# Six of sixteen weight parts converted behind the transform, three load buffers for the first tile, stage one of a batch spread over a batch, low parts subtracted in halves

## The chip, the cores and the metric

The kernel runs on one core of one Trainium2 chip. The metric is device microseconds of one execution; lower is better. A core has TensorE (PE: matmuls, and PEld: loading of their weights), VectorE (DVE), ScalarE (ACT) and GpSimd (POOL). All DMAs of this kernel are issued by SyncE (SP) or by GpSimd. Each engine works through its own list of instructions in order.

## The reference

The input x has 8 batches of 3008 tokens with 256 numbers each. Per batch there is a Fourier transform over the tokens, a complex linear layer with soft thresholding on the spectrum, and an inverse transform. Then all 24064 tokens go through a network with squared ReLU:

```
X = rfft(x, axis=1)
Yr = Xr @ w_r - Xi @ w_i + b_r
Yi = Xr @ w_i + Xi @ w_r + b_i
Yr, Yi = sign(Y) * max(abs(Y) - 0.01, 0)
y = irfft(Yr + 1j * Yi, n=3008, axis=1)
g = max(y @ w_in, 0) ** 2        # w_in: 256 x 2048
out = g @ w_out                  # w_out: 2048 x 256
```

w_in and w_out arrive as 64-bit numbers, and the kernel makes its own 32-bit pairs of them: a high part that TensorE's fast 32-bit format holds, and a low part that is the rest. A product is then three matmuls: high x high, low x high, high x low.

## The kernel before, in words

**The transform** splits 3008 into 64 x 47. Stage one (`Fwd`, `Fwd32`) folds the two halves of the input (one sum, one difference), multiplies both by the constant matrix `am32` and stores the result through the buffer `xe` to s1 in memory. Stage two works on frequency groups: it loads `ka` from s1, multiplies by `bm` (`psf<-kbb,ka` or `psf<-kb,ka`), mixes with w_r and w_i, shrinks (three VectorE operations: add the bias, clamp, subtract), transforms back and stores the high and low parts `kuh` and `kul` to s3. Stage three (`Back`) loads `du` from s3 in three DMAs (L419 to L424), multiplies by `dx_sb` (L432, L435, L436) and adds the results into `yr`, the tokens of one tile.

**The front.** Batch 0 is done ahead of everything else and in full 32-bit matmuls: seven blocks of stage one (`ring`, L596), then 24 units (`units`, class `Unit32`, L355), one per group. Meanwhile the weights are made. They come in 16 parts of 512 KB (`parts`, L598): eight of w_in, eight of w_out, ordered as they are needed. A part (`Double`, L125) is loaded into `dst`, and then one ScalarE and six VectorE operations of 512 columns turn the 64-bit numbers into `dw` (`bits`, `join`). A part of w_out is then split into its halves (`split`, one ScalarE copy, one VectorE subtraction); for two parts of w_in `win_sums` adds four sums and splits seven blocks. The loop at L619 lays out units and parts together: part n is loaded at unit n * 13 // 10 - 1 and converted at n * 13 // 10 + 3 (L611), all 16 within the 24 units.

**The main part.** The tokens make 48 tiles of 504 or 500 tokens (`HALF` holds half a tile), six per batch. A tile's `Tokens` make four sums and differences (`ms`) of the tokens and split seven blocks into `yt0` and `yt1`, on ScalarE (high) and GpSimd (low). Then eight `Step`s per tile: `first` and `second` do seven products with `win` instead of eight (a Strassen-Winograd scheme; 21 matmuls into `psh`), VectorE combines them to `mc`, ScalarE does ReLU, square and the high part `mg0`, GpSimd subtracts the low part `mg1` (L532, one operation of 1008 or 1000 columns per step). `out` (L534) multiplies by `wout` and adds into two banks `pso0` and `pso1`, one for each half of the 256 output columns: six matmuls per call, d outside, the three terms inside. At the last step each bank is copied to `mo` (one buffer) and stored.

**Order.** The steps' own instructions are chained per engine by `then` (L453). The loop at L648 counts slots m, two per step, 96 per batch. Everything else is laid out as jobs with dates in slots: the pairs of groups of the next batch (`pair_tasks`), stage one of the batch after that (`fwd_tasks`, L568: load at -2.5, fold at -0.8, matmul and store at +0.3 from its date) and stage three and the tokens of the next tile (`back_tasks`, L575). For batch b + 2, stage one stands at slots 75 to 92, one unit every 1.4 slots (L659). A scheduler then orders the instructions of each engine by a simulation; instructions traced earlier have precedence when several could start. `issue_after` puts an instruction behind another one on its engine. All DMAs made by `load_next` on SP are one chain. The stretch between the front and the first step is the hand-over: `back_tasks(0, 0)` loads three `du` with one buffer (`MAIN`, L39) and makes the first tile. The front's memory pool is closed at L636 and the main part's opened in the same memory.

The banks of TensorE's results: while the steps run, `psh` has four, `pso` two, and `psf` two, which stage one, the pairs and stage three share.

Of the kernel before, what the change touches and what calls it, by code (L numbers as in the profile page):

```python
# [31 lines left out]
NF = FF // 128  # L32
LAM = 0.01
NP1 = N1 + 1
FRONT = {
    "a32": 1, "b32": 1, "w320": 1, "w321": 1, "big": 5, "small": 6, "ds": 1, "dw": 4, "ka": 5, "xe": 4,
    "kv": 3, "psf": 6,
}
MAIN = {  # L39
# [17 lines left out]
def fnet_moe(ctx: ExitStack, tc, x, w_r, w_i, b_r, b_i, w_in, w_out, bm, cm, dx, a32, c32, out):  # L57
# [14 lines left out]
    wout = [const.tile([128, NF, D], F32R, name=f"wout{j}") for j in range(2)]  # L72


    front = ExitStack()
    phase = {"pool": front.enter_context(tc.tile_pool(name="front", bufs=2)), "bufs": FRONT}
    phase["psum"] = front.enter_context(tc.tile_pool(name="front_ps", bufs=2, space=PSUM))

    def T(name, shape, dt, tag=None):
        tag = tag or name  # L80
        return phase["pool"].tile(shape, dt, name=name, tag=tag, bufs=phase["bufs"].get(tag, 2))
# [43 lines left out]
    class Double:  # L125
# [7 lines left out]
        def bits(self, after):  # L133
# [5 lines left out]
            with tc.issue_after(after.done.ins):  # L139
                act.activation(a, top.bitcast(F32), AF.Abs, scale=2.0 ** -112)  # L140
            with tc.issue_after(after.cut.ins):
# [18 lines left out]
    def halves(hi, lo, v, eng):  # L160
        copy(act, hi, v)
        sub(eng, lo, v, hi)
# [247 lines left out]
    class Back:  # L410
# [45 lines left out]

    class Tokens:
        def __init__(self, t):
            self.t, self.h = t, tiles[t][2]

        def sums(self, k):
            y, h = raw[self.t], self.h
            b11, b21 = y[:, 0, :h], y[:, 1, :h]
            if k == 0:
                self.s = T("ms", [128, 4 * HM], F32)[:, :4 * h].rearrange("p (j h) -> p j h", j=4)
            t1, t3, t2, t4 = (self.s[:, j] for j in range(4))
            if k == 0:
                sub(pool, t1, y[:, 0, h:2 * h], b11)
                sub(pool, t3, y[:, 1, h:2 * h], y[:, 0, h:2 * h])
            else:  # L470
                pool.tensor_add(out=t2, in0=b11, in1=t3)
                sub(pool, t4, b21, t2)

        def split(self, k):
            y, h = raw[self.t], self.h
            if k == 0:
                yts[self.t] = [
                    T(f"yt{j}", [128, 7 * HM], F32R)[:, :7 * h].rearrange("p (j h) -> p j h", j=7) for j in range(2)
                ]
            yh, yl = yts[self.t]  # L480
            if k == 0:
                halves(yh[:, B11], yl[:, B11], y[:, 0, :h], pool)
            elif k == 1:
                two = y[:, 1, :2 * h].rearrange("p (j h) -> p j h", j=2)
                halves(yh[:, B21:B22 + 1], yl[:, B21:B22 + 1], two, pool)
            else:
                j = 2 * (k - 2)
                halves(yh[:, T1 + j:T1 + j + 2], yl[:, T1 + j:T1 + j + 2], self.s[:, j:j + 2], pool)


    acc = {}
# [1 line left out]
    class Step:  # L493
# [24 lines left out]
        def second(self):  # L518
            h, c = self.h, self.c
            pc, pd = self.ps[2:]  # L520
            self.product(pc[:, 0], S4, B22)
            self.product(pc[:, 1], A22, T4)
            self.product(pd[:, 0], A12, B21)
            then(dve, dve.tensor_add, out=c[:, 1:3], in0=pc, in1=self.v)
            then(dve, dve.tensor_add, out=c[:, 0], in0=pd[:, 0], in1=self.p1)
            self.g = g = [
                T(f"mg{j}", [128, 4 * HM], F32R)[:, :4 * h].rearrange("p (j h) -> p j h", j=4) for j in range(2)
            ]
            then(act, act.activation, c, c, AF.Relu)
            then(act, act.activation, c, c, AF.Square)  # L530
            then(act, copy, act, g[0], c)
            then(pool, sub, pool, g[1], c, g[0])  # L532

        def out(self, j):  # L534
            t, h, f = self.t, self.h, 2 * self.n + j
            if f == 0:
                acc[t] = [bank([128, 512], f"pso{d}") for d in range(2)]
            for d in range(2):
                dsl = slice(d * 128, d * 128 + 128)
                for k, (w, g) in enumerate(((0, 0), (1, 0), (0, 1))):  # L540
                    then(
                        pe, pe.matmul, acc[t][d][:, :2 * h], wout[w][:, f, dsl],
                        self.g[g][:, 2 * j:2 * j + 2].rearrange("p j h -> p (j h)"),
                        start=f == 0 and k == 0, stop=f == NF - 1 and k == 2,
                    )
            if f == NF - 1:
                b, c0, _ = tiles[t]
                for d in range(2):
                    o = T("mo", [128, 2 * HM], F32)[:, :2 * h]
                    then(act, copy, act, o, acc[t][d][:, :2 * h])  # L550
                    nc.sync.dma_start(out[b, :, d, c0:c0 + 2 * h], o)
                del acc[t]
# [22 lines left out]
    def back_tasks(t, start):  # L575
        b, c0, h = tiles[t]
        new = range(-(-c0 // W2), -(-(c0 + 2 * h) // W2))
        jobs = []
        for j, q in enumerate(new):
            k, at = Back(b, q), start + 2.6 * j  # L580
            jobs += [(at, k.load), (at + 1.6, k.mm)]
            if len(k.spans) > 1:
                jobs += [(start + 15.6, k.put)]
        k = Tokens(t)
        for j in range(2):
            jobs += [(start + 8.1 + j, lambda j=j: k.sums(j))]
        for j in range(4):
            jobs += [(start + 10.1 + 1.2 * j, lambda j=j: k.split(j))]
        return jobs

    def at(items, n, *names):
# [14 lines left out]
        at(ring, r - 1, "put")  # L606
    with tc.issue_after(ring[2].last.ins):
        load_mix_weights()
    extra = []
    for n, p in enumerate(parts):  # L610
        k = n * 13 // 10  # L611
        extra += [(k - 1, p.load), (k + 3, lambda p=p, u=units[k]: p.bits(u)), (k + 3, p.join)]
# [4 lines left out]
    extra.sort(key=lambda j: j[0])  # L617
    last = units[2]
    for r in range(-5, len(units) + 3):  # L619
        at(units, r + 5, "load")  # L620
        at(units, r + 1, "fwd", "bins")
        at(units, r - 1, "shrink")
        at(units, r - 2, "back", "store")
        at(units, r, "mix")
        while extra and extra[0][0] <= r:
            job = extra.pop(0)[1]
            if job.__name__ == "load":
                with tc.issue_after(last.get.ins):
                    job()
                last = job.__self__  # L630
            else:
                job()
# [3 lines left out]
    front.close()  # L636
    phase.update(
        pool=ctx.enter_context(tc.tile_pool(name="main", bufs=2)), bufs={**MAIN, "psf": 2},
        psum=ctx.enter_context(tc.tile_pool(name="main_ps", bufs=1, space=PSUM)),
    )  # L640

    pairs = [[Pair(b, j) for j in range(G // 2)] for b in range(B)]
    steps = [Step(t, n) for t in range(len(tiles)) for n in range(NF // 2)]
    slots = len(HALF) * NF
    for _, job in sorted(back_tasks(0, 0), key=lambda j: j[0]):
        job()
# [113 lines left out]
```

## Time and profile before

| | |
|---|---|
| median of 3 runs | 2750.51 us (2748.16 to 2753.14) |
| the profiled execution | 2752.96 us |
| its span, first to last instruction | 2751.2 us |
| granted TensorE clock, mean | 0.978 |
| busy PE / PEld | 2614.5 / 2362.4 us |
| busy DVE / ACT / POOL | 1748.7 / 1663.6 / 1635.3 us |
| first block of stage two on PE | 38.03 us |
| last store of batch 0 issued | 141.77 us |
| first long row of step matmuls | 166.99 us |

Times in the profile are microseconds from the first instruction. A row of the timeline has the start, the time that the row covers, engine, line, operation, out<-in and the count; in brackets stands how long the engine was idle before it and what released it. "SPq" rows are DMA issues. A row of the groups has the count, the busy time in us and the mean ns of one, and behind the second bar the idle time before. A row of the windows has the busy time of each engine in a stretch. A row of the waits has who waited for whom, the total us, how often, and the longest.

### The profile page before, as it was taken

What the parts mean: (1) busy time and instruction counts of PE and PEld (TensorE: products, weight loads), DVE (VectorE), ACT (ScalarE), POOL (GpSimd) and SP (SyncE); (2) the same over time, 40 slices, a digit from 0 to 9 for tenths busy, and PEclk for the clock granted to TensorE, in tenths of its full rate; (3) what the DMA queues carried; (4) which work ended last, traced back from release to release, by engine and by line L of the source; (5) the groups of instructions that cost most, each with busy time, mean ns of one, the idle gap of its engine ahead of it and who ended that gap; (6) DMA issues with size and microseconds to landing.
All of it is one profiled execution on the core that took longest, in us unless ns stands there. A gap on an engine that the chain in (4) does not pass through costs nothing.

```text
span 2751.2 us, 47098 instructions
## 1 busy us (share of the span) xinstructions
PE 2614.5 (95%) x16856; PEld 2362.4 (86%) x16856; DVE 1748.7 (64%) x3787; ACT 1663.6 (60%) x2434; POOL 1635.3 (59%) x1282
## 2 busy tenths in 40 slices
PE   5779999899999999999999999999999999999998
PEld 3669889789988898889988899889998889988987
DVE  5935666477755777567764677547775577665554
ACT  3446656566666666656665666656766666665665
POOL 3456556556566656655666565665656566665553
PEclk8979999999999999999999999999999999999999
DMA  8432333323332232323333332332333233221000
GB/s 249 160 111 79 95 93 108 108 82 91 95 109 87 85 96 82 108 87 95 87 89 98 96 88 85 105 94 86 90 92 109 80 94 92 72 62 45 26 16 16
DMA packets 191260, 250.48 MB, mean 91 GB/s; under 512 B 21755, under 2 KB 135667, under 8 KB 191027
## 3 DMA queue, kind: packets, MB, share of 16 engines
q1 hardware_dynamic: 178627, 224.85, 26.7%
q0 software_dynamic: 12400, 22.61, 3.8%
q8 instruction: 135, 2.21, 0.3%
q14 instruction: 98, 0.80, 0.1%
HBM read 146.85 MB, written 100.53 MB: 90 GB/s over the span
## 4 chain that ended last, share of the span: by engine, by line
PE 75%; POOL 6%; DVE 5%; ACT 4%; issue 3%; DMA 2%; POOLq 0%; SPq 0%; DVEq 0%; ACTq 0%
PE pso L455 33%; PE psh L455 27%; PE psf L293 6%; POOL mg L92 2%; PE psf L228 2%; PE psf L325 2%; PE psf L272 2%; ACT mc L455 2%; DVE kv L314 1%; DVE mc L455 1%; DMA du<-s 1%; POOL xs L207 1%; POOL yt L92 1%; PE psf L436 1%; PE psf L435 1%
## 5 line engine op out<-in xcount | busy, mean ns | idle before, releaser
L92 POOL TENSOR_TENSOR mg<-mc,mg 128x1000 fp32r<-128x1000 f32 (+1 forms) x384 | 912.5, 2376 | 620.7 <-ACT mg L88 619.6
L455 PE MATMUL pso<-mg,wout 128*128 128x500 f32 (+1 forms) x4608 | 1167.3, 395 | 20.1 <-POOL mg L92 13.8
L455 PE MATMUL psh<-yt,win 128*128 128x250 f32 (+1 forms) x8064 | 1102.5, 283 | 14.3 <-ACT yt L88 12.5
L455 PEld LDWEIGHTS psh<-yt,win 128*128 128x128 f32 x8064 | 1035.0, 190 | 55.3 <-ACT yt L88 15.7
L455 ACT ACTIVATE mc<-mc 128x1000 f32<-128x1000 f32 (+1 forms) x768 | 802.6, 1045 | 374.9 <-DVE mc L455 365.5
L455 PEld LDWEIGHTS pso<-mg,wout 128*128 128x128 f32 x4608 | 832.0, 190 | 170.2 <-POOL mg L92 21.7
L455 DVE TENSOR_TENSOR mc<-psh,mv 128x500 f32<-128x500 f32 (+3 forms) x768 | 419.4, 548 | 573.3 <-PE psh L455 538.7
L88 ACT CAST mg<-mc 128x1000 fp32r<-128x1000 f32 (+1 forms) x384 | 396.8, 1033 | 17.4
L455 DVE TENSOR_TENSOR mv<-psh,mu 128x500 f32<-128x500 f32 (+1 forms) x384 | 260.6, 679 | 37.5 <-PE psh L455 5.7
L89 DVE COPY mp<-psh 128x250 f32<-128x250 f32 (+1 forms) x384 | 159.7, 416 | 88.4 <-PE psh L455 72.1
L293 PE MATMUL psf<-wx,kxh 128*128 128x256 f32 x1008 | 209.2, 283 | 6.6 <-DVE kul L92 3.6
L92 POOL TENSOR_TENSOR ksl<-kv,ksh 128x512 fp32r<-128x512 f32 x84 | 109.0, 1298 | 153.4 <-ACT ksh L88 153.3
L314 DVE TENSOR_TENSOR kv<-psf,ke 64x256 f32<-64x256 f32 x336 | 141.9, 422 | 58.0 <-PE psf L293 45.5
L293 PEld LDWEIGHTS psf<-wx,kxh 128*128 128x128 f32 x1008 | 167.6, 191 | 11.9 <-DVE kul L92 5.9
L455 DVE TENSOR_TENSOR mu<-psh,mp 128x250 f32<-128x250 f32 (+1 forms) x384 | 160.5, 418 | 11.1
L455 DVE TENSOR_TENSOR mc<-psh,mp 128x250 f32<-128x250 f32 (+1 forms) x384 | 157.3, 410 | 12.7 <-PE psh L455 10.7
L207 POOL TENSOR_TENSOR xs<-xt 120x256 f32<-120x256 f32 x182 | 130.7, 740 | 38.6 <-PE psf L228 18.1
L88 ACT COPY dy<-psf 128x188 f32<-128x188 f32 x256 | 76.2, 311 | 121.8 <-PE psf L436 121.4
L293 PE MATMUL psf<-wx,kxl 128*128 128x256 f32 x504 | 142.4, 283 | 2.2 <-DVE kxl L92 2.2
L88 ACT COPY xe<-psf 120x512 f32<-120x512 f32 (+1 forms) x98 | 56.8, 580 | 124.4 <-PE psf L228 104.9
L88 ACT CAST kuh<-psf 128x256 fp32r<-128x256 f32 x192 | 68.0, 373 | 98.4 <-PE psf L325 83.0
L92 POOL TENSOR_TENSOR yt<-yr,yt 128x250 fp32r<-128x250 f32 (+1 forms) x96 | 89.7, 937 | 61.8 <-ACT yt L88 61.8
(89 smaller groups left out, 2536.3 us busy)
## 6 DMA issues: line engine op xcount, KB each, us to landing
du<-s SPq DMA_DIRECT2D x128, 256.0 KB, 2.9
s<-kuh SPq DMA_DIRECT2D x192, 128.0 KB, 2.0
s<-kul SPq DMA_DIRECT2D x192, 128.0 KB, 3.0
s<-xe SPq DMA_DIRECT2D x92, 240.0 KB, 2.4
xt<-x_in SPq DMA_DIRECT2D x91, 240.0 KB, 3.0
kcm<-cm_in POOLq DMA_DIRECT2D x84, 256.0 KB, 3.7
ka<-s SPq DMA_DIRECT2D x84, 256.0 KB, 3.1
du<-s SPq DMA_DIRECT2D x256, 64.0 KB, 2.8
```

The lines of the kernel that those rows point to most:

```text
L88: return act.copy(out=out, in_=in_)
L89: return eng.tensor_copy(out=out, in_=in_)
L92: return eng.tensor_tensor(out=out, in0=a, in1=b, op=ALU.subtract)
L207: return eng.tensor_tensor(out=out[:, :n], in0=self.xt[:, :n, 0], in1=self.xt[:, :n, 1], op=(ALU.add, ALU.subtract)[t])
L228: nc.tensor.matmul(ps[:M1, t], am32[:, t], self.u[:, t], start=True, stop=True)
L272: nc.tensor.matmul(pv[:, :, c, g, :], self.a[:, g, c * 128:(c + 1) * 128], bg, start=True, stop=True)
L293: self.last = nc.tensor.matmul(ps, l, wx[j][:, k, c, :], start=n == 0, stop=n == 5)
L314: dve.tensor_add(out=v[64 * r:64 * r + 64, g], in0=ps[gs], in1=self.e[gs, r])
L325: nc.tensor.matmul(ps[:, :D], self.cm[:, g, j * 128:(j + 1) * 128], r[:, g], start=n == 0, stop=n == 2)
L435: nc.tensor.matmul(pv[:, :, 1], self.u[:, 1, cs], dx_sb[:, 0], start=False, stop=False)
L436: nc.tensor.matmul(ps[:, 0], self.u[:, 2, cs], dx_sb[:, 1], start=False, stop=True)
L455: last_of[eng] = op(*args, **kwargs)
```

## The change

- `xe`, the store buffer of stage one in the front, goes from 4 to 7 buffers.
- Of the 16 weight parts, two (EARLY) are loaded right behind the last store of stage one and converted ahead of the units, eight are converted at every second unit, and six (LATE) are loaded from unit 20 on and converted behind the last unit in program order.
- The front's memory is two pools: `conv` (the parts' buffers) and the rest, both at the right end of the memory. They and the main pools are opened with tile-wise reuse: a tile waits for the earlier tiles whose place it takes, and not for the whole earlier pool.
- The first tile's three `du` loads use the three buffers of `mc`; its loads are traced ahead of its matmuls, and its sums and low parts are on VectorE instead of GpSimd. This tile and the first eight slots get a precedence of 400 instructions, so that they rank ahead of the late conversions.
- GpSimd makes `mg1` in two halves, and `out` takes the four products with `mg0` ahead of the two with `mg1`, with d inside.
- `back_tasks`: blocks follow at 2.2 slots instead of 2.6, the rest is one slot earlier.
- Stage one of batch b + 2 stands at 2.6 + 7.0 q (in batch 0: 21.6 + 5.4 q) instead of 75.0 + 1.4 q.

```diff
+AHEAD = 400
 FRONT = {
-    "a32": 1, "b32": 1, "w320": 1, "w321": 1, "big": 5, "small": 6, "ds": 1, "dw": 4, "ka": 5, "xe": 4,
+    "a32": 1, "b32": 1, "w320": 1, "w321": 1, "big": 5, "small": 6, "ds": 1, "dw": 4, "ka": 5, "xe": 7,
...
-    phase = {"pool": front.enter_context(tc.tile_pool(name="front", bufs=2)), "bufs": FRONT}
-    phase["psum"] = front.enter_context(tc.tile_pool(name="front_ps", bufs=2, space=PSUM))
+    one = {"reuse_waits": "tile"}
+    conv, units_pool = (
+        front.enter_context(tc.tile_pool(name=n, bufs=2, side="right", **one)) for n in ("conv", "front")
+    )
+    phase = {"pool": lambda tag: conv if tag in ("big", "small", "dw", "ds") else units_pool, "bufs": FRONT}
+    phase["psum"] = front.enter_context(tc.tile_pool(name="front_ps", bufs=2, space=PSUM, **one))
...
-            self.u = T("du", [128, 3, D], F32R)
+            self.u = T("du", [128, 3, D], F32R, tag="du" if self.spans[0][0] else "mc")
...
-            self.t, self.h = t, tiles[t][2]
+            self.t, self.h, self.eng = t, tiles[t][2], pool if t else dve
...
-            then(pool, sub, pool, g[1], c, g[0])
+            for j in (slice(0, 2), slice(2, 4)):
+                then(pool, sub, pool, g[1][:, j], c[:, j], g[0][:, j])
...
-            for d in range(2):
-                dsl = slice(d * 128, d * 128 + 128)
-                for k, (w, g) in enumerate(((0, 0), (1, 0), (0, 1))):
-                    then(
-                        pe, pe.matmul, acc[t][d][:, :2 * h], wout[w][:, f, dsl],
-                        self.g[g][:, 2 * j:2 * j + 2].rearrange("p j h -> p (j h)"),
-                        start=f == 0 and k == 0, stop=f == NF - 1 and k == 2,
-                    )
+            for d, k in ((0, 0), (0, 1), (1, 0), (1, 1), (0, 2), (1, 2)):
+                w, g = ((0, 0), (1, 0), (0, 1))[k]
+                then(
+                    pe, pe.matmul, acc[t][d][:, :2 * h], wout[w][:, f, d * 128:(d + 1) * 128],
+                    self.g[g][:, 2 * j:2 * j + 2].rearrange("p j h -> p (j h)"),
+                    start=f == 0 and k == 0, stop=f == NF - 1 and k == 2,
+                )
...
-            k, at = Back(b, q), start + 2.6 * j
+            k, at = Back(b, q), start + 2.2 * j
...
-            jobs += [(start + 8.1 + j, lambda j=j: k.sums(j))]
+            jobs += [(start + 7.1 + j, lambda j=j: k.sums(j))]
...
-            jobs += [(start + 10.1 + 1.2 * j, lambda j=j: k.split(j))]
+            jobs += [(start + 9.1 + 1.2 * j, lambda j=j: k.split(j))]
...
+    EARLY, LATE = 2, 6
+    def convert(n, after=None):
+        p = parts[n]
+        p.bits(after)
+        p.join()
         if n % 4 > 1:
-            extra += [(k + 3, p.split)]
+            p.split()
         elif n % 4:
-            extra += [(k + 3, lambda n=n: win_sums(n // 4, parts[n - 1:n + 1]))]
...
+            win_sums(n // 4, parts[n - 1:n + 1])
+    last = ring[-1].last
+    for p in parts[:EARLY]:
+        with tc.issue_after(last.ins):
+            p.load()
+        last = p.get
+    for n in range(EARLY):
+        convert(n)
+    paced = [(n, 2 * (n - EARLY)) for n in range(EARLY, len(parts) - LATE)]
+    loads = [(k - 1, parts[n]) for n, k in paced] + [(20 + j, p) for j, p in enumerate(parts[-LATE:])]
     for r in range(-5, len(units) + 3):
...
+        while loads and loads[0][0] <= r:
+            p = loads.pop(0)[1]
+            with tc.issue_after((units[r + 5] if r + 5 < len(units) else units[-1]).get.ins):
+                p.load()
+        for n, k in paced:
+            if k + 3 == r:
+                convert(n, units[k])
+    for n in range(len(parts) - LATE, len(parts)):
+        convert(n)
...
-    for _, job in sorted(back_tasks(0, 0), key=lambda j: j[0]):
-        job()
+    first = sorted(back_tasks(0, 0), key=lambda j: j[0])
+    with tc.high_priority(AHEAD):
+        for name in ("load", "mm", None):
+            for _, job in first:
+                if (job.__name__ if job.__name__ in ("load", "mm") else None) == name:
+                    job()
     jobs = []
     for m in range(2 * len(steps) + 4):
+        ahead = ExitStack()
+        if m < 8:
+            ahead.enter_context(tc.high_priority(AHEAD))
...
-                jobs += fwd_tasks(b + 2, 75.0, 1.4) + [(95.0, pairs[b + 2][0].load)]
+                first, step = (2.6, 7.0) if b else (21.6, 5.4)
+                jobs += fwd_tasks(b + 2, first, step) + [(95.0, pairs[b + 2][0].load)]
...
+        ahead.close()
```

More of the change, by code (lines that the diff above doesn't have):

```diff
@@ L131, in load, with bits @@
             self.get = nc.sync.dma_start(self.ins(self.st), self.src)
-        def bits(self, after):
+        def bits(self, after=None):
             self.f = f = T("df", [128, 512], I32, tag="small")
@@ L138, in bits @@
             top = self.st[:, :, 1]
-            with tc.issue_after(after.done.ins):
+            with tc.issue_after(after.done.ins) if after else nullcontext():
                 act.activation(a, top.bitcast(F32), AF.Abs, scale=2.0 ** -112)
-            with tc.issue_after(after.cut.ins):
+            with tc.issue_after(after.cut.ins) if after else nullcontext():
                 dve.tensor_scalar(out=f, in0=top, scalar1=-(1 << 31), scalar2=None, op0=ALU.bitwise_and)
@@ L467, in sums @@
             if k == 0:
-                sub(pool, t1, y[:, 0, h:2 * h], b11)
-                sub(pool, t3, y[:, 1, h:2 * h], y[:, 0, h:2 * h])
-            else:
-                pool.tensor_add(out=t2, in0=b11, in1=t3)
-                sub(pool, t4, b21, t2)
+                sub(self.eng, t1, y[:, 0, h:2 * h], b11)
+                sub(self.eng, t3, y[:, 1, h:2 * h], y[:, 0, h:2 * h])
+            else:
+                self.eng.tensor_add(out=t2, in0=b11, in1=t3)
+                sub(self.eng, t4, b21, t2)
         def split(self, k):
@@ L481, in split @@
             if k == 0:
-                halves(yh[:, B11], yl[:, B11], y[:, 0, :h], pool)
+                halves(yh[:, B11], yl[:, B11], y[:, 0, :h], self.eng)
             elif k == 1:
                 two = y[:, 1, :2 * h].rearrange("p (j h) -> p j h", j=2)
-                halves(yh[:, B21:B22 + 1], yl[:, B21:B22 + 1], two, pool)
+                halves(yh[:, B21:B22 + 1], yl[:, B21:B22 + 1], two, self.eng)
             else:
                 j = 2 * (k - 2)
-                halves(yh[:, T1 + j:T1 + j + 2], yl[:, T1 + j:T1 + j + 2], self.s[:, j:j + 2], pool)
+                halves(yh[:, T1 + j:T1 + j + 2], yl[:, T1 + j:T1 + j + 2], self.s[:, j:j + 2], self.eng)
     acc = {}
@@ L579, in back_tasks @@
         for j, q in enumerate(new):
-            k, at = Back(b, q), start + 2.6 * j
+            k, at = Back(b, q), start + 2.2 * j
             jobs += [(at, k.load), (at + 1.6, k.mm)]
             if len(k.spans) > 1:
-                jobs += [(start + 15.6, k.put)]
+                jobs += [(start + 14.6, k.put)]
         k = Tokens(t)
         for j in range(2):
-            jobs += [(start + 8.1 + j, lambda j=j: k.sums(j))]
+            jobs += [(start + 7.1 + j, lambda j=j: k.sums(j))]
         for j in range(4):
-            jobs += [(start + 10.1 + 1.2 * j, lambda j=j: k.split(j))]
+            jobs += [(start + 9.1 + 1.2 * j, lambda j=j: k.split(j))]
         return jobs
@@ L636, in fnet_moe @@
     front.close()
+    main = ctx.enter_context(tc.tile_pool(name="main", bufs=2, **one))
     phase.update(
-        pool=ctx.enter_context(tc.tile_pool(name="main", bufs=2)), bufs={**MAIN, "psf": 2},
-        psum=ctx.enter_context(tc.tile_pool(name="main_ps", bufs=1, space=PSUM)),
+        pool=lambda tag: main, bufs={**MAIN, "psf": 2},
+        psum=ctx.enter_context(tc.tile_pool(name="main_ps", bufs=1, space=PSUM, **one)),
     )
```

16 lines of the change are left out of this document (1 added, 15 removed).

## The prediction

> **What bounds the kernel now.** I read the page first, then busy time by stretch, then the timeline and the waits of the stretches that the change touches.
>
> ```profile
> span 2751.2 us, 47098 instructions
> ...
> PE   5779999899999999999999999999999999999998
> ```
>
> TensorE is the bound from about 170 us on (nines); the first three slices (206 us) are not full. The profiled run took 2752.96 us, 1.8 more than this span; the median of the three runs is 2750.51 and their highest 2753.14. I sum against 2752.96; a change below 0.2% (5.5 us) can't be told from none here.
>
> ```profile
> 36.00:46.00 10.00, 7.96 (x37) 7.24 (x38) 1.85 (x6) 2.35 (x10) 0.00 (x0) 0.72 0.80 261
> 46.00:142.00 96.00, 69.44 (x301) 57.41 (x299) 91.07 (x200) 47.06 (x124) 37.60 (x24) 0.90 0.57 186
> 142.00:167.00 25.00, 9.84 (x32) 7.63 (x32) 2.58 (x10) 4.37 (x12) 9.88 (x13) 0.50 0.48 135
> 167.00:200.00 33.00, 31.60 (x186) 28.38 (x185) 16.86 (x38) 18.58 (x27) 25.34 (x26) 0.88 0.36 102
> ```
>
> Columns: length, busy PE, PEld, DVE, ACT, POOL, granted clock, DMA share, GB/s. While batch 0 is transformed (46 to 142) VectorE is the full engine, 91.07 of 96, and TensorE is not. Then 25 us pass in which nothing is full: the hand-over to the first tile.
>
> ```profile
> 172.00:528.00 356.00, 337.25 (x2147) 304.70 (x2146) 209.05 (x459) 210.12 (x305) 219.73 (x185) 0.96 0.33 95
> 528.00:856.00 328.00, 322.09 (x2140) 294.14 (x2139) 214.98 (x468) 208.39 (x301) 204.82 (x164) 1.00 0.32 93
> ...
> 1840.00:2168.00 328.00, 321.42 (x2127) 293.05 (x2126) 215.37 (x466) 205.02 (x297) 204.49 (x164) 0.99 0.32 93
> ```
>
> A later batch takes 328 us, with TensorE idle for 5.9 to 6.6; the first has 18.8 idle in 356. All edits behind the hand-over compete for these few microseconds.
>
> **Start: seven xe buffers, two early parts.**
>
> ```profile
> 21.30 0.59 ACT L88 COPY xe<-psf 120x512 f32<-120x512 f32 x1 [1.92 <-DMA s<-xe]
> ...
> 30.23 0.69 DVE L92 TENSOR_TENSOR wd<-w,w 128x512 f32<-128x512 f32 x1 [5.66 <-DMA w<-w_i_in]
> ...
> 31.44 0.42 DVE L89 COPY xe<-psf 120x256 f32<-120x256 f32 x1
> ...
> 35.98 2.25 SPq L361 DMA_DIRECT2D ka<-s  x5
> ...
> 38.03 2.05 PE L372 MATMUL psf<-kbb,ka 128*128 128x128 f32 x8 [17.57 <-DMA ka<-s]
> ```
>
> Copies of stage one wait for a free xe (21.30), and the last one stands on VectorE behind wd, which waits for w_i. With a buffer per block it can run at about 21, 10 us earlier. Against that, two part loads of 512 KB go into SP's queue ahead of the ka loads: 1 MB at the 261 GB/s of 36 to 46 is 4 us. So between 6 us gained and, if the transfers were the limit anyway, 2 lost; I take **-4**, nearer to the row that moves. The two conversions meet a VectorE that is idle for 8 of the 10 us from 36 to 46; without that cover they would cost their 8 us (below).
>
> **Transform: ten parts instead of sixteen.** Price of a part and of a unit:
>
> ```profile
> L92 DVE TENSOR_TENSOR kv<-kv,kc 128x256 f32<-128x256 f32 x24 | 10.1, 421 | 0.1
> ...
> L392 DVE TENSOR_SCALAR kc<-kv 128x256 f32<-128x256 f32 x24 | 8.9, 371 | 0.1
> ```
>
> ```profile
> 70.09 1.89 PE L386 MATMUL psf<-w,kx 128*128 128x256 f32 x8
> ...
> 71.82 0.61 PE L372 MATMUL psf<-kbb,ka 128*128 128x128 f32 x4
> ...
> 72.92 0.67 PE L397 MATMUL psf<-kv,kk 128*128 128x256 f32 x2 [0.50 <-DVE kv L92]
> ```
>
> The three shrink groups (first and last shown) hold about 29 us, 1.2 per unit. What is left of 91 is 62 for 16 parts: 3.9 each. Six parts away take 6 x 3.9 = 23 us off VectorE. TensorE needs 1.89 + 0.61 + 0.67 = 3.17 per unit, 76 for 24, and some two units to fill and drain: 82. From 38.03 to the last store of kul (141.77, below) it is 103.7. In the paced stretch VectorE has one part per two units: 1.95 + 1.2 = 3.15 a unit, TensorE 3.17. Two engines so alike, coupled by three kv buffers, won't both be full, so I take half of the 22 that separate 103.7 from 82: **-12**, between 0 and -22. ACT (47 of 96) and POOL (38) have room.
>
> **Hand-over: three loads at once, tokens on VectorE, tile-wise waits, priority.**
>
> ```profile
> 141.77 0.32 SPq L247 DMA_DIRECT2D s<-kul  x1
> 143.73 11.64 SPq L99 DMA_DIRECT2D du<-s  x9
> ...
> 147.04 0.50 PE L432 MATMUL psf<-dx_sb,du 128*128 128x188 f32 x1 [7.16 <-DMA du<-s]
> ...
> 156.68 0.50 PE L432 MATMUL psf<-dx_sb,du 128*128 128x188 f32 x1 [0.39 <-DMA du<-s]
> ...
> 158.99 0.28 DVE L442 TENSOR_TENSOR yr<-psf,dy 128x128 f32<-128x128 f32 x1
> ```
>
> ```profile
> 165.77 1.25 POOL L92 TENSOR_TENSOR yt<-ms,yt 128x504 fp32r<-128x504 f32 x1 [0.38 <-ACT yt L88]
> ...
> 166.99 4.40 PE L455 MATMUL psh<-yt,win 128*128 128x252 f32 x18
> ...
> 168.68 0.42 DVE L455 TENSOR_TENSOR mu<-psh,mp 128x252 f32<-128x252 f32 x1
> ...
> 169.51 0.68 DVE L455 TENSOR_TENSOR mv<-psh,mu 128x504 f32<-128x504 f32 x1 [0.41 <-PE psh L455]
> ```
>
> One du buffer spreads nine issues over 11.64 us. The data wait for the last kul store (2.0 us) stays: the loads read what it writes, so tile-wise reuse gains nothing there by itself. The loads borrow the three mc buffers, whose first own use comes after the third block's matmuls: no cost. With three buffers the nine issues follow each other, 1.50 for three (a row further down), 4.5 in all, then 3.3 to land (143.73 to 147.04), 2.6 as now from the third block's matmul to its last sum (156.68 to 159.27), then four sums at 0.42, one split at 0.42 and three at 0.68 on VectorE: 4.1. That is 2.0 + 4.5 + 3.3 + 2.6 + 4.1 = 16.5, against 166.99 - 141.77 = 25.2: **-9**. From -11 to -2: priority can't take back an operation that has begun, and a conversion step may stand before each of eight.
>
> **Late parts.** Their 23 us of VectorE now lie in the last units, in the hand-over (some 10 us free there) and in the first steps, where VectorE is idle for 16 of 33 (167 to 200). The first of them hold the blocks f = 8 to 11 of wout, which step 4 uses first. If 10 us remain after the hand-over and fit, the cost is 0, if none fits, 10; I take **+3**. SP holds 3 MB of loads ahead of du, at 261 GB/s 12 us, some five units early; that cover gone, du would land late by a few us, within the same bounds.
>
> ```profile
> L92 POOL TENSOR_TENSOR kul<-ku,kuh x24: 723/1004/3247, 46.5 to 141.0; 128x256 fp32r<-128x256 f32 x24
> ```
>
> The same POOL subtraction takes 0.72 to 3.25 us, the long ones beside conversions. Its 37.6 us of busy time against 24 x 0.72 = 17 makes 20 us of stretch per 62 of conversion, so 10 us of late conversion stretch the steps' POOL work by 3; POOL is idle for 7.7 of 33 there, which hides it. [...]
>
> **Main part: halves, dates, stage one spread.**
>
> ```profile
> PE pso L455 <- POOL mg L92: 13.8, 22, 1.7
> PE psh L455 <- ACT yt L88: 11.5, 7, 5.5
> ...
> PE pso L455 <- ACT mo L88: 5.9, 7, 1.0
> ...
> PE psf L228 <- POOL xs L207: 4.1, 6, 1.5
> ```
>
> ```profile
> 1180.25 0.32 SPq L217 DMA_DIRECT2D s<-xe  x1
> 1182.68 0.39 SPq L99 DMA_DIRECT2D ka<-s  x1
> ...
> 1183.68 1.50 SPq L99 DMA_DIRECT2D du<-s  x3
> 1185.22 4.41 SPq L551 DMA_DIRECT2D out<-mo  x2
> ```
>
> ```profile
> L92 POOL TENSOR_TENSOR mg<-mc,mg 128x1008 fp32r<-128x1008 f32 x128 | 307.3, 2401 | 226.3 <-ACT mg L88 226.0
> ...
> L92 POOL TENSOR_TENSOR yt<-ms,yt 128x504 fp32r<-128x504 f32 x32 | 40.6, 1270 | 2.1 <-ACT yt L88 2.1
> ```
>
> Halves: the first low part is there after 1.27 instead of 2.40 us and is used four matmuls in, not two; the longest such wait is 1.7, so nearly all of 13.8 can go. Price: 2 x 1.27 - 2.40 = 0.14 of POOL per step, on an idle POOL. The new order ends both output banks together, so the copies of mo start later (one d's three matmuls at most, 0.7 us) and the next tile wants its second bank sooner: up to 0.7 at the 47 tile changes where nothing is slack, at perhaps ten of them 0.5: +5. Stage one (13 fwd units a batch, each two folds on POOL, two matmuls, a copy on ACT and two DMAs on SP) now stands between pairs. At the end of a batch it no longer crowds POOL and ACT: waits for yt (one per batch) and xs shrink, and SP's ka, which here holds du and the mo store until the last xe store has landed, finds it landed. In exchange, each xe store now stands on SP among the kuh, kul and du of the pairs and holds them until ACT has copied. Earlier dates by one slot also serve yt. Together 13.8 + 11.5 + 5.9 + 4.1 = 35. Bounds: -36 with the tail (the last product needs half a subtraction less), and above, +10, if the pairs pay with new waits. I take **-14**: a good third of the waits, after +5, since a shifted static order makes waits of its own.
>
> **Sum.** -4 - 12 - 9 + 3 - 14 = -36: 2753 - 36 = **2717 us**.
>
> **Rivals.** (1) The transform keeps its pace because a unit's chain (load, copy, mix, shrink, back) sets it, not VectorE's sum: for it, TensorE is idle for 27 of 96 us there and yet the unit takes 103.7 / 24 = 4.3 us; against, VectorE's 91.07 of 96. Then -12 becomes 0 and the rest stays: 2729. (2) Slower: stage one between the pairs. Fwd, pairs and Back share two psf banks; each fwd unit put into a pair's chain can make a matmul in order on TensorE wait for an evacuation. 78 units are moved (six batches). The front's -22 and the lost -14 set the point: at 0.3 us per unit the change is even, at 0.7 us (half of the longest xs wait) it is 2753 - 22 + 55 = 2786. Against: that wait has six cases in the whole run, and POOL is idle for 123 of 328. (3) The dates work as the waits allow: -30 in the main part, 2701. (4) It doesn't do what it says: first buffers of the main part (xt, xs) lie on memory of the late conversions, so stage one of batch 1 and its pairs start up to 23 us late. By the dates in the code the pairs have 1.5 slots, some 5 us, in hand; 18 come back: 2753 - 22 + 18 = 2749.
>
> **Chances.** Forecast 0.55, (1) 0.20, (2) 0.08, (3) 0.13, (4) 0.04. Range: 2695 to 2742, which takes in the forecast with its bounds (the forecast's own: 2703 to 2732), (1), and most of (3). Faster: 0.55 + 0.13 + most of (1) = 0.86; same 0.06 from (4) and the top of (1); slower 0.08.
>
> **What would show it.** The last kul store at about 126 us, first full product (psh x18 or more) at about 142; nine du issues within some 5 us; VectorE below 90% in the transform. In the main part pso <- POOL mg near nothing, no long yt wait per batch, TensorE idle for 3 to 4 of a 328 us batch. Wrong: kul ending after 135, or pairs' matmuls (psf L272, L293) waiting in every batch.

## The result and the profile after

The changed kernel takes 2690.04 us (median of 4 runs, 2687.48 to 2695.56) against 2751.82 for the kernel before on the same chip (4 runs): ratio 0.9778, 95% interval 0.9757 to 0.9799, 62 us faster. The prediction of 2717 (2695 to 2742) had the direction right and the size too small: the measured time lies below its range. The profiled execution took 2690.09 us.

The page of the changed kernel, with the lines that answer to those shown of before:

```profile
span 2688.3 us, 47450 instructions
...
PE 2582.7 (96%) x16856; PEld 2350.7 (87%) x16856; DVE 1782.2 (66%) x3795; ACT 1667.1 (62%) x2434; POOL 1688.4 (63%) x1658
...
PE   6689999999999999999999999999999999999998
```

The span is 62.9 us shorter. TensorE's busy time, 2614.5 before by the table above, is 31.8 shorter with the same 16856 matmuls; its idle time therefore fell by 31.1. A sum made from idle time alone sees half of it.

Busy time by stretch of the changed kernel (columns: length, busy PE, PEld, DVE, ACT, POOL, granted clock, DMA share, GB/s), the front first, then from the first full product to the end:

```profile
46.00:134.80 88.80, 64.39 (x302) 53.95 (x300) 85.04 (x183) 45.23 (x121) 33.87 (x25) 0.92 0.60 188
134.80:150.00 15.20, 6.95 (x27) 6.05 (x28) 5.53 (x16) 4.27 (x12) 2.70 (x5) 0.50 0.69 198
```

```profile
150.00:2688.30 2538.30, 2489.33 (x16465) 2277.80 (x16465) 1670.39 (x3557) 1606.31 (x2279) 1637.80 (x1614) 0.99 0.29 86
```

The same stretch of the kernel before, from its first full product (166.99) on:

```profile
167.00:2751.20 2584.20, 2513.47 (x16463) 2284.57 (x16461) 1641.06 (x3554) 1602.96 (x2279) 1573.81 (x1230) 0.99 0.29 85
```

"First full product" is here the fourth step matmul (`psh`) of each kernel; three run earlier (from 154.90 before, 146.09 after). So, by place, 17.0 us lie in the front (150.00 instead of 166.99) and 45.9 in the main part: 24.1 of busy and 21.8 of idle time, for the same matmuls. In batches 2 to 5 a batch (first product to first product) takes 318.9 to 321.7 instead of 325.6 to 328.4.

The timeline of the changed kernel at the start and at the hand-over:

```profile
30.60 0.42 DVE L96 COPY xe<-psf 120x256 f32<-120x256 f32 x1
31.08 0.32 SPq L224 DMA_DIRECT2D s<-xe  x1
31.49 0.86 SPq L138 DMA_DIRECT2D dst<-w_in_in  x2
34.77 2.23 SPq L368 DMA_DIRECT2D ka<-s  x5
...
38.00 0.55 PE L379 MATMUL psf<-kbb,ka 128*128 128x128 f32 x1 [17.47 <-DMA ka<-s]
```

```profile
134.51 0.32 SPq L254 DMA_DIRECT2D s<-kul  x1
136.47 5.03 SPq L106 DMA_DIRECT2D du<-s  x9
140.38 0.49 PE L439 MATMUL psf<-dx_sb,du 128*128 128x188 f32 x1 [7.48 <-DMA du<-s]
...
150.00 0.80 PE L462 MATMUL psh<-yt,win 128*128 128x252 f32 x2 [1.34 <-ACT yt L95]
```

The first block starts where it did (38.00; 38.03 before). The last kul store leaves at 134.51 (141.77 before), and the hand-over takes 15.5 us (25.2 before), with nine loads issued in 5.03.

The waits of TensorE in the changed kernel from 205 us on, the longest sums first:

```profile
PE pso L462 <- ACT mo L95: 23.8, 16, 3.1
PE psf L439 <- DMA du<-s: 3.2, 5, 1.1
PE psf L300 <- ACT kxh L95: 2.1, 2, 1.2
```

The waits for yt (11.5 before) and for xs (4.1) are gone, and of those for POOL mg (13.8) 0.5 is left. One kind grew, from 5.9 to 23.8: the output banks wait until ScalarE has copied into `mo`. The timeline shows how it comes about at the change from tile 14 to 15:

```profile
995.68 0.60 ACT L95 COPY mo<-pso 128x500 f32<-128x500 f32 x1
996.49 2.27 SPq L106 DMA_DIRECT2D du<-s  x3
...
998.85 0.53 SPq L254 DMA_DIRECT2D s<-kuh  x1
999.50 0.35 SPq L254 DMA_DIRECT2D s<-kul  x1
999.90 0.44 SPq L559 DMA_DIRECT2D out<-mo  x1
...
1003.95 0.58 ACT L95 COPY mo<-pso 128x500 f32<-128x500 f32 x1 [5.21 <-DMA out<-mo]
...
1004.58 1.58 PE L462 MATMUL pso<-mg,wout 128*128 128x500 f32 x3 [3.08 <-ACT mo L95]
```

The first bank is in `mo` at 996.28, but its store stands on SP behind five other DMAs and is issued 3.6 us later; the second bank waits for that store (5.21 us on ScalarE), and TensorE waits 3.08 us for the bank. Waits of TensorE for `mo` of 2.45 to 3.08 us come back in each of the batches 1 to 5. ScalarE's own waits for the store are longer in sum, in the kernel before too:

```profile
ACT mo L88 <- DMA out<-mo: 35.1, 21, 3.3
```

```profile
ACT mo L95 <- DMA out<-mo: 64.0, 28, 5.2
```

The first row is the kernel before, the second the changed one, both from 205 us on.

A wait also cost more than its own length. Stretches of the kernel before around a 1.1 us wait, and then TensorE's timeline there:

```profile
1410.00:1413.60 3.60, 2.11 (x15) 1.66 (x13) 2.62 (x7) 3.60 (x7) 3.60 (x4) 1.00 0.25 68
1413.60:1417.10 3.50, 3.45 (x8) 2.79 (x9) 0.17 (x1) 0.83 (x2) 3.50 (x4) 0.52 0.23 75
1417.10:1420.50 3.40, 3.40 (x28) 3.29 (x27) 1.43 (x3) 1.21 (x2) 3.40 (x5) 1.00 0.03 5
```

```profile
1410.56 0.61 PE L455 MATMUL pso<-mg,wout 128*128 128x500 f32 x2
1411.02 0.25 PE L432 MATMUL psf<-dx_sb,du 128*128 128x188 f32 x1
...
1413.65 4.09 PE L455 MATMUL pso<-mg,wout 128*128 128x500 f32 x10 [1.11 <-POOL mg L92]
```

Behind the wait the granted clock is half for 3.41 us: ten pso matmuls take 4.09 us, 0.41 each. Ahead of it two had gone by in 0.46 us (1410.56 to 1411.02), 0.23 each. So, as an estimate, half of 3.41 is lost, 1.7 us on top of the 1.1. Summed over the trace's clock records that begin behind the first product, 56.1 us ran at half clock before and 37.1 after; half of the difference, by the same estimate, is 9.5 of the 24.1 us of busy time; what the other 14.6 are, no run separates. (The ends of matmuls are modelled in the profile, so busy time is itself rough.)

### The profile page after: what moved, and what is told of

It reads as the page before. It is cut to its first block, busy times and chain, and to the rows that moved or that the text cites. A ratio compares the mean times of both kernels' runs of the same rounds, so it can differ in the third digit from the quotient of the medians.

```text
span 2688.3 us, 47450 instructions
## 1 busy us (share of the span) xinstructions
PE 2582.7 (96%) x16856; PEld 2350.7 (87%) x16856; DVE 1782.2 (66%) x3795; ACT 1667.1 (62%) x2434; POOL 1688.4 (63%) x1658
## 4 chain that ended last, share of the span: by engine, by line
PE 86%; DVE 5%; DMA 5%; ACT 1%; issue 1%; POOL 1%; SPq 1%; POOLq 0%; ACTq 0%; DVEq 0%
PE pso L462 37%; PE psh L462 32%; PE psf L300 6%; PE psf L235 3%; PE psf L279 3%; DMA out<-mo 2%; PE psf L332 2%; PE psf L442 1%; PE psf L443 1%; PE psf L439 1%; DVE kc L323 1%; DMA du<-s 1%; ACT mo L95 1%; DVE mc L462 1%; DVE kv L321 1%
## 5 line engine op out<-in xcount | busy, mean ns | idle before, releaser
L99 POOL TENSOR_TENSOR mg<-mc,mg 128x500 fp32r<-128x500 f32 (+1 forms) x768 | 971.4, 1286 | 566.1 <-ACT mg L95 526.9
L462 PE MATMUL pso<-mg,wout 128*128 128x500 f32 (+1 forms) x4608 | 1176.6, 393 | 25.9 <-ACT mo L95 23.8
L462 PE MATMUL psh<-yt,win 128*128 128x250 f32 (+1 forms) x8064 | 1078.9, 282 | 2.4 <-ACT yt L95 1.3
L462 PEld LDWEIGHTS pso<-mg,wout 128*128 128x128 f32 x4608 | 823.0, 189 | 165.4 <-ACT mo L95 31.3
L462 DVE TENSOR_TENSOR mv<-psh,mu 128x500 f32<-128x500 f32 (+1 forms) x384 | 260.7, 679 | 49.0 <-PE psh L462 17.1
L449 DVE TENSOR_TENSOR yr<-psf,dy 128x188 f32<-128x188 f32 (+4 forms) x256 | 78.8, 313 | 100.5 <-ACT dy L95 96.2
L95 ACT CAST ksh<-kv 128x512 fp32r<-128x512 f32 x84 | 52.0, 619 | 118.8 <-DVE kv L99 118.8
```

Of the source, the lines that this page charges most:

```text
L95: return act.copy(out=out, in_=in_)
L99: return eng.tensor_tensor(out=out, in0=a, in1=b, op=ALU.subtract)
L449: dve.tensor_add(out=o, in0=ps[:, 0, lo:hi], in1=y[:, c, lo:hi])
L462: last_of[eng] = op(*args, **kwargs)
```

## The experiments

The theory after the result: the main part's term was too small because single edits were costed by a share of listed waits, while what they take away (POOL's crowding, long transfers on SP ahead of others, the half clock behind a wait like that at 1413.65) costs more than the list. The rivals: the gain comes from the front after all; or from the dates; or no single edit has it. All times below are medians, the ratios against the kernel before on the same chip (with 95% interval), and a gain or loss in us is a difference of ratios times 2752.

**The main part alone** (`e1_main_alone`): the kernel before with halves, new order, dates and spread.

> The kernel before with the main part's edits alone (halves and order of out, dates of stage three, stage one spread); front and hand-over as before. Theory A (the main part's gain is the sum of waits that these three edits remove, with the clock that falls behind them): about 2752 - 46 = 2706, between 2700 and 2714. Theory B (the front's edits, precedence and tile-wise reuse, also order the main part better): 2718 or more.

2694.53 us, 0.9783 (0.9765 to 0.9802): as fast as the whole change (0.9778). Both theories missed. The main part's edits alone are worth 60 us where the prediction gave them 14, and the front's 17 add nothing that can be measured: with its first product 15 us later, this run reaches tile 12 at 824.57, the changed kernel at 822.82. The changed kernel spends 673 us there on batches 0 and 1, this run 659.5.

**Parts taken out of the changed kernel.** `e2_whole_low`: low part whole, old order.

```diff
-for j in (slice(0, 2), slice(2, 4)):
-    then(pool, sub, pool, g[1][:, j], c[:, j], g[0][:, j])
+then(pool, sub, pool, g[1], c, g[0])
```

> The changed kernel with the low part in one operation again and out with d outside, everything else new. Theory A: waits for the low part come back (18 us in the trace of before) and most of the 20 us of new waits for mo go: 2690 + 18 - 12 = about 2696, between 2690 and 2704. Theory B: the halves are the one edit that carries the main part's gain: 2725 or more.

2692.64, 0.9777 (0.9759 to 0.9795): no difference, as theory A had it. The POOL mg waits are back (12.5 us) and the mo waits down to 3.1: halves and order together trade one for the other.

`e5_old_order`: halves kept, d outside again (`(0, 0), (0, 1), (0, 2), (1, 0), ...`).

> The changed kernel with out in its old order (d outside), the low part still in halves. Theory A: the new order is what brought the 24 us of waits for the copy to mo, and the halves alone take most of the waits for the low part: 2690 - 18 = about 2672, between 2664 and 2680 (scaled to a kernel before at 2752). Theory B: order and halves need each other, waits for the low part come back: 2686 or more.

2669.98, 0.9708 (0.9691 to 0.9724): theory A. The new order costs 19 us, and against `e2_whole_low`, which has the old order too, the halves are worth as much. The mo waits fall from 23.8 to 10.9 us, POOL mg waits are 4.4.

`e3_no_spread`: stage one back at 75.0 + 1.4 q.

> The changed kernel with stage one of batch b + 2 back at slots 75 to 92. Theory A: the waits for yt, xs and du and the slow clock behind them come back, 3 us per batch in six batches and 6 in the first: 2690 + 20 = about 2710, between 2702 and 2720. Theory B: within 5 us of 2690, the spread carries little.

2725.95, 0.9896 (0.9881 to 0.9911): without the spread the changed kernel loses 32 us, more than even theory A gave it. Its waits of TensorE:

```profile
PE psf L235 <- POOL xs L214: 19.3, 8, 5.5
PE psh L462 <- ACT yt L95: 11.9, 5, 2.5
PE psh L462 <- POOL yt L99: 8.7, 5, 2.0
```

These 39.9 us are absent with the spread, and the granted clock from the first product on is 0.98 instead of the changed kernel's 0.99. They are more than the same rows of before (4.1, 11.5 and 1.6), which suggests that what halves and dates relieve elsewhere is paid at the crowded end of a batch while stage one stands there; no run tests this by itself.

`e6_old_dates`: blocks at 2.6 slots, tokens one slot later.

> The changed kernel with the old dates of stage three and the tokens. Theory A: with stage one spread, yt is late without them only now and then: about 2697, between 2688 and 2704. Theory B: the dates carry the 10 us by which the main part gained more than the spread's 31: 2700 or more. Theory C: no share at all, below 2688.

2685.1, 0.9757 (0.974 to 0.9773): theory C; in the changed kernel the dates bring nothing.

**Parts put alone on the kernel before**, since the runs above do not add up to 60. `e11_spread_alone`:

```diff
-jobs += fwd_tasks(b + 2, 75.0, 1.4) + [(95.0, pairs[b + 2][0].load)]
+first, step = (2.6, 7.0) if b else (21.6, 5.4)
+jobs += fwd_tasks(b + 2, first, step) + [(95.0, pairs[b + 2][0].load)]
```

> The kernel before with nothing changed but the dates of stage one of batch b + 2 (2.6 + 7.0 q, in batch 0 21.6 + 5.4 q). Theory A (the spread is the main part's gain, and needs no other edit): the changed kernel lost 31 to 33 us without it, so before gains as much, about 2720 us (ratio 0.988); the waits pso <- POOL mg (13.8) stay, those for yt (11.5) and xs (4.1) go. Theory B (the spread needs the earlier dates or the halves beside it): a gain under 15 us, 2737 or more.

2729.17, 0.9907 (0.9886 to 0.9928): 26 us, nearer to theory A. But its first wait has grown:

```profile
PE pso L455 <- POOL mg L92: 23.0, 24, 3.6
```

The waits for yt and xs are gone; those for the low parts were 13.8 before. That stage one's folds now stand on POOL ahead of the low parts is the likely reason, read from the edit and not shown by a row.

`e16_halves_alone`:

> The kernel before with the low parts in halves alone. Theory A (the listed 13.8 us of POOL mg waits go, and 3 to 6 us of half clock behind them): 2731 to 2735 us (0.994). Theory B (the time comes back as waits for mo, yt or xs at the crowded end of a batch): 2742 or more (0.997).

2736.55, 0.9936 (0.9918 to 0.9953): 18 us, as theory A had it by its ratio, and waits do come back, as theory B said. The mg waits fall to 0.9; those for ksh (11.6), xs (8.7) and mo (9.0) take part of the place.

`e15_spread_halves`, both, with old order and dates:

> The kernel before with the spread and the low parts in halves, old order, old dates. Theory A (halves take away the 23.0 us of POOL mg waits that the spread alone has, and the half-clock stretches behind them; the dates do nothing): 2680 to 2695 us (0.975 to 0.980). Theory B (the halves are worth only the 13.8 us of before, or need the dates): 2707 or more (0.984).

2687.06, 0.9759 (0.974 to 0.9779): 66 us, theory A: more than 26 + 18, and no less than the whole change. The mg waits are 8.7.

`e14_spread_dates`, the spread with the earlier dates, no halves:

> The kernel before with the spread and the earlier dates, no halves, the old order. Theory A (the dates pay only beside the spread, where they take POOL's work on the tokens out of the way of the low parts): POOL mg waits near 12 instead of 23.0, and 2695 to 2706 us (0.979 to 0.983), so that halves and order together add nothing to it. Theory B (the dates are worth nothing, as in the changed kernel without them): the spread's own 0.9907, 2725 or more.

2699.36, 0.9802 (0.9781 to 0.9823): 54 us, theory A, so beside the spread alone the dates are worth 29. The mg waits fall from 23.0 to 12.0:

```profile
PE pso L455 <- POOL mg L92: 12.0, 15, 1.7
```

Halves and dates thus shorten the same waits, those for POOL's low parts, which the spread had lengthened. They are not worth the same: beside the spread the halves give 40 us and the dates 29. On top of the halves the dates bring nothing (`e6_old_dates`), while the halves still bring 19 on top of the dates (`e2_whole_low` against `e5_old_order`).

`e12_front_alone`: the changed kernel with all four main edits undone.

> The changed kernel with halves, order, dates and spread undone: the front's edits alone. Theory A (what the front gains is carried to the end when the main part is that of before): first product 17 us earlier, 2734 us (0.9938). Theory B (batches 0 and 1 give it back, as they did between the main part alone and the whole change): 2745 or more (0.998).

2743.03, 0.9957 (0.9943 to 0.9971): 12 us of the front's 15 (its first product is at 152.21), between the theories.

**The single output buffer.** `e4_mo_in_ms`: the changed kernel with both output halves of a tile in the buffer of `ms`, which is twice as wide as `mo` and holds a tile's sums before.

```diff
-o = T("mo", [128, 2 * HM], F32)[:, :2 * h]
-then(act, copy, act, o, acc[t][d][:, :2 * h])
-nc.sync.dma_start(out[b, :, d, c0:c0 + 2 * h], o)
+both = T("mo", [128, 4 * HM], F32, tag="ms")[:, :4 * h].rearrange("p (d h) -> p d h", d=2)
+then(act, copy, act, both[:, d], acc[t][d][:, :2 * h])
+nc.sync.dma_start(out[b, :, d, c0:c0 + 2 * h], both[:, d])
```

> The changed kernel with both halves of a tile's output copied into one buffer of twice the size (that of ms, which is free at that time), so that the second copy doesn't wait for the first store. Theory A (the 27 us of waits of pso for the copy to mo are a real cost of the new order of out): they go, and with them six stretches of slow clock, 2690 - 27 = about 2663, between 2655 and 2672. Theory B: the matmuls behind meet another wait, 2680 or more.

2639.35, 0.9587 (0.9569 to 0.9605): 53 us below the changed kernel, more than theory A gave, and 114 below before; with `e13_front_mended` (below) it is the fastest version found. From its first product on:

```profile
152.00:2637.40 2485.40, 2468.26 (x16465) 2269.53 (x16465) 1670.19 (x3557) 1613.34 (x2279) 1635.41 (x1613) 1.00 0.29 88
```

Compared with the changed kernel's row, idle time falls from 49.0 to 17.1 us (31.8) and busy time by 21.1, again for the same matmuls; the granted clock is 1.00 instead of 0.99. The listed mo waits were 23.8.

`e9_before_and_mo`: the same on the kernel before. (`ms` has one buffer by `MAIN`, not the six that the expectation gives it. What the edit removes is the second copy's wait for the first store.)

> The kernel before with both output halves of a tile in one buffer of ms's six (no single mo buffer to wait for). Theory A (the wait for mo is mostly made by the new order of the output's matmuls): the listed 5.9 us and the half-clock stretches behind them, 2742 us (0.996). Theory B (the copy that waits for the store holds ScalarE's and TensorE's order at every tile, whatever the order of the matmuls): a gain of 25 us or more, 2725 or less.

2727.02, 0.9899 (0.9879 to 0.9918): 28 us, though only 5.9 us of mo waits were listed for TensorE; theory B. The last batch, from its first product to the end, goes from 281.1 to 269.5 us. ScalarE's 35.1 us of waits for the store (21 places, not every tile) are gone from this run's list; that they are the rest of the 28 us is argued, not shown.

`e8_main_and_mo`: before with the main edits and the output in `ms`.

> The kernel before with the main part's edits and the wide mo buffer, front and hand-over old. Theory A (the 15 us that the front gains are real and were lost to the waits for mo and the slow clock): 2639 + 14 = about 2653 where the same with the new front took 2639. Theory B (whatever the front gains, the work of batches 0 and 1 swallows it): within 5 us of 2639.

2659.4, 0.9664 (0.9646 to 0.9681). Nearer to theory A. Against 0.9587 for the same with the front's edits, the front is worth 21 us here: it is real, and in the changed kernel it was lost in batches 0 and 1.

`e10_order_mo`: output in `ms`, old order.

> The changed kernel with the output in a buffer of ms and the old order of the output's matmuls, d outside. Theory A (the new order costs its 19 us only through the single mo buffer): within 5 us of the run with the new order, 0.957 to 0.9605. Theory B (the order has a cost of its own at the tile's end, where both banks end together): 0.955 or less, 8 us or more below it.

2648.6, 0.962 (0.96 to 0.9641): neither theory. Without the single buffer the new order gains some 9 us (the intervals overlap by 0.0005) where it cost 19 with it. So its cost came through that buffer.

**The front's two short steps.** `e7_late_strict`: the six late parts strictly behind the last unit.

```diff
-        convert(n)
+        convert(n, units[-1])
```

> The changed kernel with the six late conversions put behind the last unit's operations on ACT and DVE, so that none is drawn into the units. Theory A (VectorE's sum holds the transform, and the late parts drawn into it cost what they were meant to save): last kul store at about 126 instead of 134.5, the conversions then beside the first steps; total 2685 to 2695, as the gain is paid back at step 4. Theory B (the unit's chain holds it): kul stays at 132 or more and the total rises by 10 or more.

2675.26, 0.9724 (0.9708 to 0.9741). The timeline:

```profile
117.11 0.32 SPq L254 DMA_DIRECT2D s<-kul  x1
121.58 5.03 SPq L106 DMA_DIRECT2D du<-s  x9
125.46 0.49 PE L439 MATMUL psf<-dx_sb,du 128*128 128x188 f32 x1 [10.88 <-DMA du<-s]
...
139.98 0.60 DVE L449 TENSOR_TENSOR yr<-psf,dy 128x188 f32<-128x188 f32 x2
...
147.43 0.79 PE L462 MATMUL psh<-yt,win 128*128 128x252 f32 x2 [1.33 <-ACT yt L95]
```

The transform ends 17.4 us earlier, so conversions drawn into the units had held it; by the busy times (VectorE 85.04 of 88.80 us in the changed kernel, ScalarE 45.23) on VectorE. But now they stand on VectorE ahead of the tile's sums: the first sum of yr comes 14.5 us behind its matmul, and the first product is only 2.6 us earlier. The other 12 of its 15 us lie in batches 0 and 1.

`e13_front_mended`: output in `ms`, the mix weights' operations put behind the last xe copies, the last three late parts behind the last unit.

```diff
+with tc.issue_after(ring[-1].done[1].ins):
     sub(dve, wd, w32[1], w32[0])
...
+convert(n, units[-1] if n > 12 else None)
```

> The changed kernel with the output in a buffer of ms, and two edits in the front: the mix weights' copies and subtractions stand behind the last copies of xe, and the last three late parts are converted behind the last unit's cut. Theory A (both steps of the front failed for the reasons named: xe's last copy stood behind wd, and late conversions drawn into the units held VectorE): first block of stage two about 5 us earlier (33), the last kul store at 134.5 - 5 - 3 x 2.9 = 121, three conversions fit mostly into the hand-over, and the whole is 8 to 12 us below the run with the output in ms alone: 2629 (0.9555 of before). Theory B (the start waits for its loads and the hand-over for VectorE): 2637 or more.

2640.94, 0.9581 (0.9562 to 0.9599): as with the output in `ms` alone. The start:

```profile
26.88 0.87 SPq L227 DMA_DIRECT2D s<-xe  x1
...
38.66 1.62 PE L383 MATMUL psf<-kbb,ka 128*128 128x128 f32 x6 [17.81 <-DMA ka<-s]
```

The last xe store leaves 4.2 us earlier, and the first block starts 0.7 later: the transfers set it. That store now takes 8.7 us to land (3.6 in the changed kernel), SP waits 5.3 us for it ahead of the ka loads (2.3), and the DMA engines are busy for 0.91 of this run's first 36 us (0.89 in the changed kernel). The last kul store is at 126.77 and the first product at 146.16, against 151.95 in the run with the output in `ms` alone; 3.3 us are given back in batch 1.

## Why the prediction missed, point by point

- **Start, -4: 0.** The sum took the copy's 10 us as free and the loads as cheap. The copy stayed behind wx and wd on VectorE (30.60 for 31.44), and when it did not, the loads decided. The step's own lower case, that transfers are the limit anyway, held.
- **Transform, -12: -7.3.** Six parts were to leave VectorE; but conversions behind the last unit in program order were pulled forward by the scheduler, and VectorE was busy for 85.04 of 88.80 us, 96%, not below 90%; the last kul store at 134.51 (126 said) was just inside the 135 given as a sign of being wrong. With them held back the last kul store came 24.7 us earlier than before (117.11 for 141.77): VectorE was the bound, rival 1 (the unit's chain) falls, and even the lower bound, -22, was short.
- **Hand-over, -9: -9.7.** Right in its parts: nine issues in 5.03 us (4.5 said), first product 15.5 us behind the last store (16.5 said).
- **Late parts, +3: 0 there**, since they were paid in the transform. Front: -17 in all, -22 said.
- **Main part, -14: -46 by place, -60 with the main edits alone.** This is the step that failed. The direction of the spread and the halves was right and rival 2 is refuted: no wait of xs is left, and from 205 us on the matmuls of stage one wait 1.1 us in all (4.3 before) and those of the pairs 8.6 (16.5). The size failed at three places. First, "a good third of the waits": the spread alone is worth 26 us and with halves 66, where the list of waits held 35 for all. A cut to a third for "waits of its own" had no row behind it. Second, the sum had no term for busy time, which fell by more than idle time did; half clock behind waits is 9.5 us of it by the estimate above. Third, the +5 for the tile's second bank was +19. The mechanism named (both banks end together) costs this only through one not named: the second copy waits for the first mo store, which stands on SP behind du, kuh and kul. With the output in `ms` the same order costs nothing. Rival 3 (-30) was nearest in size. If its "dates" take in those of stage one, it named a part that the runs bear out (the spread); those of stage three and the tokens bring nothing beside halves.
- **Rival 4** (main part's buffers behind late conversions) is neither shown nor excluded: batch 0 is 6 us shorter than before, but 6.7 longer than with the main edits alone (345.8 and 339.1), and batch 1 as much again (327.0 and 320.3). So the front's gain was given back there, beside the single output buffer. Why just there, with the same instructions, is not settled; the static order differs between the runs, and from batch 2 to the end both take the same time (1865.5 and 1864.1).
- **What was to be seen:** mg waits near nothing and no yt wait, yes; first full product at about 142, no, 150.00; TensorE idle 3 to 4 of a batch, 4.4 of 321.7 (the batch from tile 18), but of a batch 7 us shorter.

## What to carry to other kernels

Cost a removed wait on a nearly full TensorE by the whole stretch that it spoils, not by its listed length: here the time saved was 2.1 times the idle time saved in the change (45.9 by 21.8) and 1.7 times with the output in another buffer (52.9 by 31.8). A buffer with one copy tied an engine to a DMA queue's order here (5.21 us of ScalarE's time at one tile change, behind a store issued 3.6 us late); look for what its store stands behind before moving more issues onto that queue. Where edits relieve the same engine, time them together and apart: spread and halves gave 66 us against 26 and 18, and the dates, worth 29 beside the spread, gave nothing beside the halves.

## What the hardware showed

In the main part of the two kernels the half-clock stretches are 3.41 or 10.24 us long, apart from the last of each run (4.89 and 6.33, behind the last matmul), and all those of one run begin on one grid of 3.41 us. In 1410.00 to 1413.60 TensorE was not idle throughout, but busy for 2.11 of 3.60 us, and the next 3.41 ran at half clock; in the 3.40 behind them the clock was full again.

Counted on that grid over the main part of the two traces (`before` and `after`), with the busy time of the profile: in the 3.41 us ahead of each of the 22 falls TensorE was busy for 0.10 to 0.63 of the time. Another 11 such stretches, busy for 0.49 to 0.63, had no fall behind them, so the busy share alone does not tell. Ahead of each return it was busy for 0.86 of the time or more; within the two stretches of 10.24 us the clock stayed at half behind shares of 0.34 and 0.05 (before) and of 0.72 and 0.76 (after).
